# Spectral mixing in groups (0,1,2), (3), (4,5), (6,7), with its sums and the swapped weights' differences on VectorE instead of GpSimd

## The chip, the core and the metric

The kernel runs on one core of one Trainium2 chip. The metric is the time of one execution on the device. Before the change it is 1936.89 us, the median of three runs (1936.51 to 1940.29). Five engines work side by side, each through its own queue of instructions in order: TensorE (PE; its weight loads PEld stand apart in the profile), VectorE (DVE), ScalarE (ACT), GpSimd (POOL) and SyncE (SP), which here only issues DMAs.

## The reference

Three layers follow each other, on 8 batches of 576 tokens with 512 channels (4608 tokens in all):

```python
# layer 1: attention, keys and values averaged over 8 tokens
scores = scale * np.matmul(q, k_p.transpose(0, 1, 3, 2))
x = softmax(scores) @ v_p
# layer 2: mixing over tokens of rank 32, then two matmuls over channels
u = x + (x.T @ U @ V).T
x = u + np.maximum(u @ w_ch1, 0.0) @ w_ch2
# layer 3: real part of the FFT over tokens and channels, then again two matmuls
mixed = np.real(np.fft.fft(np.fft.fft(x, axis=1), axis=2))
u = x + mixed
un = (u - mean(u)) / np.sqrt(var(u) + 1e-06)
out = u + np.maximum(un @ w_ch1, 0.0) @ w_ch2        # other weights than layer 2
```

The weights come in as 64-bit floats.

## The kernel before

**Numbers in two parts.** A matmul operand is kept as a high part (rounded by ScalarE) and a low part (the difference). `split` (L105) does both: a copy on ScalarE, then the subtraction on VectorE, or on the engine it is given. So one product takes three matmuls.

**Stage one (to about 1095 us).** Attention for all batches, token mixing, and the channel layer of layer 2 in 18 blocks of 256 tokens (`st1`, `st2`, 16 slices `f` each, L1097 on). What a block finishes goes to the DRAM tensor `x1d`. TensorE's first matmul of a slice writes a bank `h0` or `h1`; VectorE then forms `low` (L917) and `hl` (L918) from it, and the bank is free again after `low`.

**Stage two (from about 1095 us).** The channel layer of layer 3, in 9 blocks of 512 tokens (`NBA`, L1207), each in 8 steps `p` (L1209) of seven products. Between the products `tick` (L1192) is called four times in every `p`. Each call steps two generators once: `d`, the spectral mixing, and `p`, the preparation of the next block. What they yield between two steps is thus put between the products in the program's order. In this stage the order of PE, DVE and ACT is the program's (L1098, L1206); before it a scheduler orders PE, DVE, POOL and SP.

**Spectral mixing (`Dft.run`, L523, called by `lane_d`, L1009).** One batch at a time, begun late in stage one (771 us) and ended in stage two (1526 us). Folded tokens: a batch's rows `F` and their mirror rows `R` are loaded in three tiles (`i` = 0, 1, 2); `S = F + R` on GpSimd (L562), then `R = F - R` and the edges `E` on VectorE. Matmuls with the tables `st` transform over tokens, those with `dt` over channels. A transformed tile goes into `S` and `E`, and four sums add it to rows loaded again (L676 to L679): two on GpSimd, two on VectorE. The result goes to the DRAM tensor `u2d`. A batch has two such output tiles of 128 rows and 33 rows that stay over. These are collected in `cath`, `catl`, `catp`, and the last batch of a group makes one further output tile of them (`n2 = 3`, L610). Only after the last batch of a group does `lane_d` say how far `u2d` goes:

```python
34    GROUPS = ((0, 1, 2), (3, 4), (5, 6, 7))
1014                  yield from df.run(b, group)
1015              state["u2"] = (group[-1] + 1) * S
```

**Preparation (`prep_a`, L765).** It loads four tiles of 128 tokens of `u2d` (`ul`), normalises each (VectorE, and GpSimd for the power, L790), transposes it on TensorE (L812), copies it back on ScalarE (L821), and splits it. In block `b`, `begin` (L1198) is asked at each `p` whether `u2` reaches to the end of block `b + 1`; only then is the preparation begun. At `p = 6` the program calls the generator again and again until it is used up, with nothing between (L1258), as the next block can't start without it.

**The swapped weights.** `w2` of layer 3 takes the place of `w2` of layer 2 at the end of stage one: `w_swap` (L246) loads one of 16 slices from `wd`, `w_swap_split` (L249) splits it, its difference on GpSimd. These are called by `swap` (L1082) in the last block of stage one and the first `p` of stage two. `ring_load` (L861) fetches the weights `wr` of the seven products.

Of the kernel before, what the change touches and what calls it, by code (L numbers as in the profile page):

```python
# [8 lines left out]
F32 = mybir.dt.float32  # L9
# [21 lines left out]
KSCALE = 1.0 / (POOL * 8)  # L31
NK = 290
NL = 258
GROUPS = ((0, 1, 2), (3, 4), (5, 6, 7))
NPR = NF // 2
TA = 512
NBA = NTOK // TA
# [7 lines left out]
def kernel(  # L45
# [18 lines left out]
    nc = tc.nc  # L64
# [25 lines left out]
    def bank(tag):  # L90
        return ps_b.tile([128, 512], F32, tag=tag, name=tag)
# [7 lines left out]
    def sub(eng, o, a, b):  # L99
        eng.tensor_tensor(out=o, in0=a, in1=b, op=ALU.subtract)  # L100

    def add(eng, o, a, b):
        eng.tensor_tensor(out=o, in0=a, in1=b, op=ALU.add)  # L103

    def split(hi, lo, src, eng=None):  # L105
        nc.scalar.activation(out=hi, in_=src, func=ACTF.Copy)  # L106
        sub(eng or nc.vector, lo, src, hi.bitcast(F32))

    def mm(o, a, b, start, stop):
        nc.tensor.matmul(o, a, b, start=start, stop=stop, skip_group_check=True)  # L110
# [137 lines left out]

    def w_swap_split(f):  # L249
        w = W[1, f]  # L250
        split(w[:, 0], w[:, 1], w[:, 1].bitcast(F32), nc.gpsimd)


    class Attn:
# [249 lines left out]
    class Dft:  # L504
# [18 lines left out]
        def run(self, b, group):  # L523
# [4 lines left out]
            def tl(tag, shape=(128, DM), dt=F32):  # L528
                return p1.tile(list(shape), dt, tag=tag, name=tag)
# [9 lines left out]
            def loads(i):  # L539
                f, r = tl("F"), tl("R")  # L540
                k0, n = KT[i]
                if i == 2:
                    for g in range(3):
                        nc.sync.dma_start(out=f[33 * g:33 * g + 33], in_=x1d[z + k0:z + k0 + 33, :])
                        nc.sync.dma_start(out=r[33 * g:33 * g + 32], in_=x1d[z + 288 + k0:z + S, :])
                        nc.sync.dma_start(out=r[33 * g + 32:33 * g + 33], in_=x1d[z + 288:z + 289, :])
                    return f, r, 99
                nc.sync.dma_start(out=f, in_=x1d[z + k0:z + k0 + n, :])
                mirror_in(r, i)
                return f, r, n  # L550
# [7 lines left out]
            for i in range(3):  # L558
                f, r, n = fr
                s = tl("S")  # L560
                e = tl("E")
                add(nc.gpsimd, s[:n], f[:n], r[:n])  # L562
                yield
                sub(nc.vector, r[:n], f[:n], r[:n])
                nc.gpsimd.tensor_copy(e[:n, 0:1], s[:n, 0:1])
                nc.gpsimd.memset(e[:n, 511:512], 0.0)
                sub(nc.vector, e[:n, 256:511], r[:n, 1:256], r[:n, 256:511])
                add(nc.vector, e[:n, 1:256], s[:n, 1:256], s[:n, 256:511])
                c2 = s[:n, 511:512].to_broadcast([n, 64])
                if i < 2:  # L570
                    fr = loads(i + 1)
                yield
                xe = tl(f"xe{i}", (128, 96 if i < 2 else 64), F32R)
                if i < 2:
                    xh, xl = tl(f"xh{i}", dt=F32R), tl(f"xl{i}", dt=F32R)
                    split(xh, xl, e)
                    nc.scalar.activation(out=xe[:, 0:64], in_=c2, func=ACTF.Copy)
                    sub(nc.vector, xe[:, 64:96], c2[:, 0:32], xe[:, 0:32].bitcast(F32))
                    X.append((xh, xl))
                    XE.append(xe)  # L580
                else:
                    m = self.sm
                    for h, y, w in ((xe, c2, 64), (None, e, 512)):
                        h = h or tl("S", dt=F32R)
                        q = r[:, 0:w]
                        nc.vector.tensor_scalar(out=q[:n], in0=y[:n], scalar1=m[:n, 0:1], scalar2=None, op0=ALU.mult)
                        nc.scalar.activation(out=h[:n], in_=y[:n], func=ACTF.Copy)
                        nc.vector.scalar_tensor_tensor(out=h[:n], in0=h[:n].bitcast(F32), scalar=m[:n, 1:2], in1=q[:n], op0=ALU.mult, op1=ALU.add)
                    X.append((h,))
                    XE.append(xe)  # L590
                yield
                if i < 2:
                    yield
                    yield
# [17 lines left out]
            def loads2(i):  # L612
                f, r = tl("F"), tl("R")
                if i < 2:
                    k0, n = KT[i]
                    nc.sync.dma_start(out=f[:n], in_=x1d[z + k0:z + k0 + n, :])
                    mirror_in(r, i)
                else:
                    n = 33 * len(group)
                    for j, zj in enumerate(y * S for y in group):  # L620
                        nc.sync.dma_start(out=f[33 * j:33 * j + 33], in_=x1d[zj + 256:zj + 289, :])
                        nc.sync.dma_start(out=r[33 * j:33 * j + 32], in_=x1d[zj + 544:zj + 576, :])
                        nc.sync.dma_start(out=r[33 * j + 32:33 * j + 33], in_=x1d[zj + 288:zj + 289, :])
                return f, r, n
# [23 lines left out]
            for i in range(n2):  # L648
                f, r, n = fr
                if i < 2:  # L650
                    k0 = KT[i][0]
                    ks = slice(k0, k0 + n)
                    Q = [(ph[:m, ks], pl[:m, ks], m) for ph, pl, m in P]
                    qx = px[:, ks]
                else:
                    hi, lo, qx = self.cat
                    Q = [(hi[:p[2], a, :n], lo[:p[2], a, :n], p[2]) for a, p in enumerate(P)]
                    qx = qx[:, :n]
                state["busy"] = True
                a, bb = bank("s0"), bank("s1")  # L660
                for c, o in ((0, a), (1, bb)):
                    for g in range(2):
                        ph, pl, m = Q[2 * c + g]
                        th, tl_ = self.dt[:m, c, g, 0], self.dt[:m, c, g, 1]
                        last = c == 1 and g == 1
                        mm(o[:n, 0:NL], ph, th, g == 0, False)
                        mm(o[:n, 0:NL], ph, tl_, False, False)
                        mm(o[:n, 0:NL], pl, th, False, last)
                mm(a[:n, 0:NL], qx, self.pt, False, True)
                s, e = tl("S"), tl("E")  # L670
                nc.scalar.activation(out=e[:n, 0:NL], in_=bb[:n, 0:NL], func=ACTF.Copy)
                sub(nc.vector, s[:n, 0:257], a[:n, 0:257], e[:n, 0:257])
                add(nc.vector, e[:n, 0:257], a[:n, 0:257], e[:n, 0:257])
                yield
                state["busy"] = False
                add(nc.gpsimd, f[:n, 0:256], f[:n, 0:256], s[:n, 0:256])  # L676
                add(nc.vector, f[:n, 256:512], f[:n, 256:512], e[:n, 1:257])
                add(nc.vector, r[:n, 0:256], r[:n, 0:256], e[:n, 0:256])
                add(nc.gpsimd, r[:n, 256:512], r[:n, 256:512], s[:n, 1:257])  # L679
                if i < 2:  # L680
                    nc.sync.dma_start(out=u2d[z + k0:z + k0 + n, :], in_=f[:n])
                if i == 0:
                    for a, m in ((1, 15), (16, 112)):
                        nc.sync.dma_start(out=u2d[z + 288 + a:z + 288 + a + m, :], in_=r[a:a + m])
                elif i == 1:
                    nc.sync.dma_start(out=u2d[z + 416:z + 544, :], in_=r)
                else:
                    for j, zj in enumerate(y * S for y in group):
                        nc.sync.dma_start(out=u2d[zj + 256:zj + 289, :], in_=f[33 * j:33 * j + 33])
                        nc.sync.dma_start(out=u2d[zj + 544:zj + 576, :], in_=r[33 * j:33 * j + 32])  # L690
                yield
                if i + 1 < n2:
                    fr = loads2(i + 1)
                    yield
                    yield
                    yield
# [312 lines left out]
    def lane_d(df):  # L1009
        for group in GROUPS:  # L1010
            for b in group:
                while state["x1"] < (b + 1) * S:
                    yield
                yield from df.run(b, group)
            state["u2"] = (group[-1] + 1) * S
# [32 lines left out]
    f = at.first()  # L1048
# [158 lines left out]
    for b in range(NBA):  # L1207
        begun = False
        for p in range(NPR):  # L1209
            x = ops[b]  # L1210
            n = 7 * (NPR * b + p)
# [157 lines left out]
```

## Time and profile before

| | before |
|---|---|
| median of 3 runs | 1936.89 us |
| the profiled execution | 1937.21 us, span 1935.4 us |
| PE busy | 1842.9 us (95%), 11239 matmuls |
| DVE busy | 1013.1 us (52%), 2281 instructions |
| ACT busy | 677.8 us (35%) |
| POOL busy | 250.4 us (13%), 387 instructions |
| DMA (q1) | 330.25 MB, 55.2% of 16 engines |
| mean granted TensorE clock | 0.985 of full speed |

The span is the time from the first to the last instruction; 1.8 us of the execution lie outside it. In the chain of work that ended last, PE has 61% of the span. In the profile's 40 slices (48.4 us each) PE's busy share is at 9 tenths or more but for four of the first five, the one from 1064 us (8) and the one from 1548 us (7); the granted clock is at 9 tenths or more but for the second (7) and the one from 1548 us (8).

### The profile page before, as it was taken

The page shows a single profiled execution, that of the slowest core. Times are in us where ns is not written, and L with a number is a line of the kernel's source. Part 1 is how long each engine was busy: PE and PEld are TensorE (multiplying, and loading weights), DVE is VectorE, ACT ScalarE, POOL GpSimd, SP SyncE. Part 2 cuts the span into 40 slices and gives each one's busy share as a digit, 9 for nine tenths or more (in the row PEclk, how much of TensorE's full clock was granted, in tenths as well). Part 3 has the DMA queues.
Part 4 walks back from the last instruction along what each step waited for, and adds up shares of the span by engine and source line. Part 5 has one row for each costly group of instructions (what it writes and reads, how often), then busy time and mean ns, then how long its engine had stood idle before and what let it go on. Part 6 is the DMA issues. An engine that isn't in the chain of part 4 may idle for free.

```text
span 1935.4 us, 31090 instructions
## 1 busy us (share of the span) xinstructions
PE 1842.9 (95%) x11239; PEld 1636.5 (85%) x11239; DVE 1013.1 (52%) x2281; ACT 677.8 (35%) x2115; POOL 250.4 (13%) x387
## 2 busy tenths in 40 slices
PE   5789899999999999999999899999999979999999
PEld 4578888898988888888888799889989968999998
DVE  8985454546454544444445755565655354444332
ACT  6553434343433432223232433333333233233221
POOL 3431011111100000111112511111111000000000
PEclk9799999999999999999999999999999989999999
DMA  9435464646453544432314758686867656757663
GB/s 363 168 124 168 137 196 142 194 134 206 121 181 108 146 118 129 117 88 57 87 49 131 251 183 260 194 266 192 252 214 247 195 153 196 238 178 226 186 211 131
DMA packets 255418, 335.64 MB, mean 173 GB/s; under 512 B 84576, under 2 KB 109248, under 8 KB 255264
## 3 DMA queue, kind: packets, MB, share of 16 engines
q1 hardware_dynamic: 254336, 330.25, 55.2%
q0 software_dynamic: 928, 3.40, 0.5%
q8 instruction: 89, 1.46, 0.3%
q14 instruction: 65, 0.53, 0.1%
HBM read 268.69 MB, written 64.88 MB: 172 GB/s over the span
## 4 chain that ended last, share of the span: by engine, by line
PE 61%; DMA 6%; DVE 4%; ACT 1%; issue 1%; SPq 1%; DVEq 0%; ACTq 0%
PE h L110 27%; PE o L110 19%; PE hu L110 5%; PE m L110 5%; PE s L110 3%; DMA cv<-w2b 3%; PE s L812 1%; DMA raw<-vr 0%; DVE hl L921 0%; DMA wr<-wc 0%; DVE xl L100 0%; DMA raw<-kT 0%; DMA ul<-u2d 0%; SPq L705 0%; DMA out<-ur 0%
## 5 line engine op out<-in xcount | busy, mean ns | idle before, releaser
L110 PE MATMUL h<-utx,w 128*128 128x256 f32 (+1 forms) x3048 | 478.8, 301 | 16.2 <-DVE hl L921 6.3
L110 PE MATMUL o<-w,hh 128*128 128x512 f32 x1632 | 478.8, 399 | 1.5 <-ACT hh L920 1.2
L110 PEld LDWEIGHTS h<-utx,w 128*128 128x128 f32 x3048 | 432.0, 192 | 56.7 <-DVE hl L921 9.9
L110 PEld LDWEIGHTS h<-x,wr 128*128 128x128 f32 x3024 | 398.0, 191 | 26.3 <-issue 2.5
L110 PE MATMUL h<-x,wr 128*128 128x256 f32 x3024 | 412.9, 284 | 5.7 <-DMA wr<-wc 2.1
L110 PEld LDWEIGHTS o<-w,hh 128*128 128x128 f32 x1632 | 289.2, 190 | 47.5 <-ACT hh L920 3.2
L110 PE MATMUL o<-w,hl 128*128 128x512 f32 x816 | 279.0, 397 | 2.5 <-DVE hl L921 2.5
L110 PEld LDWEIGHTS o<-w,hl 128*128 128x128 f32 x816 | 150.3, 190 | 28.6 <-DVE hl L921 3.8
L103 DVE TENSOR_TENSOR side<-h,side 128x256 f32<-128x256 f32 (+1 forms) x144 | 79.6, 553 | 125.7 <-PE h L110 124.3
L413 ACT ACTIVATE s<-s,mx 128x72 f32<-128x72 f32 x296 | 90.7, 332 | 69.6 <-DVE mx L410 69.5
L915 ACT ACTIVATE low<-h 128x256 f32<-128x256 f32 x102 | 39.2, 384 | 205.3 <-PE h L110 167.6
L1183 ACT ACTIVATE hh<-side 128x256 fp32r<-128x256 f32 (+1 forms) x144 | 75.0, 521 | 95.4 <-DVE side L103 88.0
L1183 ACT ACTIVATE hh<-h 128x256 fp32r<-128x256 f32 x72 | 27.6, 384 | 210.1 <-PE h L110 208.9
L1189 DVE SCALAR_TENSOR_TENSOR hl<-h,hh 128x256 fp32r<-128x256 f32 x72 | 30.5, 424 | 134.1 <-ACT hh L1183 134.1
L920 ACT ACTIVATE hh<-h 128x256 fp32r<-128x256 f32 x170 | 65.9, 387 | 97.3 <-PE h L110 88.2
L103 DVE TENSOR_TENSOR low<-h,low 128x256 f32<-128x256 f32 x102 | 42.8, 420 | 100.8 <-ACT hh L916 98.2
L1189 DVE SCALAR_TENSOR_TENSOR hl<-side,hh 128x256 fp32r<-128x256 f32 (+1 forms) x144 | 81.8, 568 | 25.1 <-ACT hh L1183 23.2
L921 DVE SCALAR_TENSOR_TENSOR hl<-h,hh 128x256 fp32r<-128x256 f32 x170 | 70.6, 415 | 34.8 <-ACT hh L920 34.3
L100 POOL TENSOR_TENSOR wo<-wo 128x256 fp32r<-128x256 f32 x56 | 43.3, 785 | 326.5 <-ACT wo L106 320.9
L110 PE MATMUL m<-w,hh 128*128 128x512 f32 x304 | 83.6, 394 | 0.0
L110 PE MATMUL hu<-w,hh 128*128 128x512 f32 x288 | 79.0, 396 | 0.0
L100 DVE TENSOR_TENSOR x<-ul,x 128x256 fp32r<-128x256 f32 x112 | 46.2, 448 | 38.5 <-ACT x L106 38.5
(254 smaller groups left out, 2423.4 us busy)
## 6 DMA issues: line engine op xcount, KB each, us to landing
wr<-wc SPq DMA_DIRECT2D x252, 512.0 KB
x<-x SPq DMA_DIRECT2D x56, 256.0 KB
wc<-wo SPq DMA_DIRECT2D x56, 256.0 KB
ur<-ud SPq DMA_DIRECT2D x36, 256.0 KB
x1d<-ur SPq DMA_DIRECT2D x36, 256.0 KB
ul<-u2d SPq DMA_DIRECT2D x36, 256.0 KB
ur<-u2d SPq DMA_DIRECT2D x36, 256.0 KB
out<-ur SPq DMA_DIRECT2D x36, 256.0 KB
```

The lines of the kernel that those rows point to most:

```text
L100: eng.tensor_tensor(out=o, in0=a, in1=b, op=ALU.subtract)
L103: eng.tensor_tensor(out=o, in0=a, in1=b, op=ALU.add)
L110: nc.tensor.matmul(o, a, b, start=start, stop=stop, skip_group_check=True)
L413: nc.scalar.activation(out=s[:n, a], in_=v[:, k], func=ACTF.Exp, bias=mx[:n, a:a + 1], accum_out=sm[:n, a:a + 1])
L812: nc.tensor.transpose(o[:, k * 128:k * 128 + 128], u[:, k * 128:k * 128 + 128], ident)
L915: nc.scalar.activation(out=low, in_=o[:, T:2 * T], func=ACTF.Copy)
L920: nc.scalar.activation(out=hh, in_=p, func=ACTF.Relu)
L921: nc.vector.scalar_tensor_tensor(out=hl, in0=p, scalar=0.0, in1=hh.bitcast(F32), op0=ALU.max, op1=ALU.subtract)
L1183: nc.scalar.activation(out=hh[:, i], in_=c, func=ACTF.Relu)
L1189: nc.vector.scalar_tensor_tensor(out=hl[:, i], in0=c, scalar=0.0, in1=hh[:, i].bitcast(F32), op0=ALU.max, op1=ALU.subtract)
```

## The change

Three edits. The mixing's groups are other ones, four in place of three: after a group's last batch `u2` now goes up after batch 2, 3, 5 and 7, where it went up after batch 2, 4 and 7. One batch more is the last of its group, so one output tile more is computed. The sum `S = F + R` and the two sums with `S` are given to VectorE, and so is the difference of the swapped weights.

```diff
-GROUPS = ((0, 1, 2), (3, 4), (5, 6, 7))
+GROUPS = ((0, 1, 2), (3,), (4, 5), (6, 7))
...
     def w_swap_split(f):
         w = W[1, f]
-        split(w[:, 0], w[:, 1], w[:, 1].bitcast(F32), nc.gpsimd)
+        split(w[:, 0], w[:, 1], w[:, 1].bitcast(F32))
...
                 s = tl("S")
                 e = tl("E")
-                add(nc.gpsimd, s[:n], f[:n], r[:n])
+                add(nc.vector, s[:n], f[:n], r[:n])
                 yield
                 sub(nc.vector, r[:n], f[:n], r[:n])
...
                 state["busy"] = False
-                add(nc.gpsimd, f[:n, 0:256], f[:n, 0:256], s[:n, 0:256])
+                add(nc.vector, f[:n, 0:256], f[:n, 0:256], s[:n, 0:256])
                 add(nc.vector, f[:n, 256:512], f[:n, 256:512], e[:n, 1:257])
                 add(nc.vector, r[:n, 0:256], r[:n, 0:256], e[:n, 0:256])
-                add(nc.gpsimd, r[:n, 256:512], r[:n, 256:512], s[:n, 1:257])
+                add(nc.vector, r[:n, 256:512], r[:n, 256:512], s[:n, 1:257])
```

What this moves is seen in the order of the instructions. First PE at `p = 6` of stage two's block 4, before. Rows with `wr` are the products, rows with `w,hh` and `w,hl` the second matmul, rows of L812 the transposes of the next block's preparation (four tiles of four).

```order
L110 MATMUL h_16522<-x_15092,wr 128x256 x6
L110 MATMUL o_16062<-w,hh 128x512 x4
L110 MATMUL o_16062<-w,hl 128x512 x2
L812 MATMUL s_16639<-ident,ul 128x128 x4
L812 MATMUL s_16655<-ident,ul 128x128 x4
L812 MATMUL s_16669<-ident,ul 128x128 x4
L812 MATMUL s_16682<-ident,ul 128x128 x4
L110 MATMUL h_16716<-x_15089,wr 128x256 x6
```

All four stand in a row, after them the first product of `p = 7`. Now the third of the four in the changed kernel, in the same block:

```order
L110 MATMUL h_16261<-x_15071,wr 128x256 x6
L110 MATMUL o_16077<-w,hh 128x512 x4
L110 MATMUL o_16077<-w,hl 128x512 x2
L812 MATMUL s_16385<-ident,ul 128x128 x4
L110 MATMUL h_16391<-x_15068,wr 128x256 x6
L110 MATMUL hu<-w,hh 128x512 x4
L110 MATMUL hu<-w,hl 128x512 x2
L110 MATMUL h_16392<-x_15476,wr 128x256 x6
```

The four are spread over block 4 from an earlier `p` on, each alone between products, as they stand in the blocks before and after it in both kernels.

Second, PE in block 0 of stage two in the changed kernel, where batch 3 is now the last of a group. `cath`, `catl`, `catp` hold the 33 rows, `s` are the two banks, `m` is the second matmul:

```order
L110 MATMUL m<-w,hh 128x512 x4
L110 MATMUL m<-w,hl 128x512 x2
L110 MATMUL s_12188<-dt,cath 33x258 x2
L110 MATMUL s_12188<-dt,catl 33x258
L110 MATMUL s_12188<-dt,cath 33x258 x2
L110 MATMUL s_12188<-dt,catl 33x258
L110 MATMUL s_12189<-dt,cath 33x258 x2
L110 MATMUL s_12189<-dt,catl 33x258
L110 MATMUL s_12189<-dt,cath 33x258 x2
L110 MATMUL s_12189<-dt,catl 33x258
L110 MATMUL s_12188<-pt,catp 33x258
L110 MATMUL h_12145<-x_11290,wr 128x256 x6
```

These 13 matmuls are new there; the tiles of the groups (4,5) and (6,7) take the place of those of (3,4) and (5,6,7).

Third, DVE near the end of stage one, before. `r` belongs to the preparation, `F`, `R`, `S`, `E` to the mixing, `low` to the channel layer:

```order
L100 TENSOR_TENSOR r_11073<-r_11207,r_11073 128x256
L100 TENSOR_TENSOR r_11073<-r_11073 128x256
L100 TENSOR_TENSOR R<-F,R 128x512
L103 TENSOR_TENSOR E<-S 128x255
L100 TENSOR_TENSOR E<-R 128x255
L103 TENSOR_TENSOR low<-h_11264,low 128x256
```

And now:

```order
L100 TENSOR_TENSOR r_11073<-r_11207,r_11073 128x256
L103 TENSOR_TENSOR S<-F,R 128x512
L100 TENSOR_TENSOR r_11073<-r_11073 128x256
L100 TENSOR_TENSOR R<-F,R 128x512
L103 TENSOR_TENSOR E<-S 128x255
L100 TENSOR_TENSOR w<-w 128x512
L100 TENSOR_TENSOR E<-R 128x255
L103 TENSOR_TENSOR low<-h_11264,low 128x256
```

Ahead of the same `low` stand two instructions more, the sum and one difference of the swapped weights. Elsewhere before stage two the scheduler's order of DVE changes by a few places; in stage two the sums stand where their generator yields them.

## Rows read from the trace of the kernel before

**Rows 1.** Windows of 50 us. Columns: stretch, us, busy (count) of each engine, clock, DMA.

```profile
1050.00:1100.00 50.00, 44.22 (x234) 37.20 (x233) 40.97 (x87) 25.64 (x67) 29.69 (x30) 0.97 0.67 210
...
1100.00:1150.00 50.00, 47.94 (x307) 43.76 (x306) 27.59 (x71) 15.89 (x39) 9.35 (x20) 0.97 0.59 203
...
1550.00:1600.00 50.00, 38.23 (x228) 33.56 (x228) 27.28 (x72) 14.65 (x36) 2.58 (x4) 0.90 0.55 168
```

**Rows 2.** Windows of 10 us, the one in the middle of the gap.

```profile
1560.00:1570.00 10.00, 3.76 (x18) 3.21 (x19) 3.37 (x12) 3.22 (x7) 0.00 (x0) 0.55 0.00 0
```

**Rows 3.** Chain of waits, 1520 to 1610 us: start, length, engine, output and line.

```profile
1537.90 1.39 PE m L110 x6
...
1548.47 1.39 PE m L110 x6
...
1555.81 0.56 DVE ul L806
1556.41 0.67 PE s L812 x4
...
1575.52 1.39 PE m L110 x6
...
1605.81 0.44 PE s L812 x4
```

**Rows 4.** Timeline of DVE, first output sum of blocks 2, 3, 4: start, length, instruction.

```profile
1379.80 0.68 DVE L103 TENSOR_TENSOR ur<-hu,ur 128x512 f32<-128x512 f32 x1
...
1475.42 0.69 DVE L103 TENSOR_TENSOR ur<-hu,ur 128x512 f32<-128x512 f32 x1 [0.57 <-PE hu L110]
...
1584.70 0.69 DVE L103 TENSOR_TENSOR ur<-hu,ur 128x512 f32<-128x512 f32 x1
```

**Rows 5.** Chain of waits of the whole span, the last group's output tile.

```profile
1519.39 1.57 PE s L110 x13
```

**Rows 6.** POOL's groups: operation, shapes, count, busy us, mean ns, idle before and releaser.

```profile
L103 POOL TENSOR_TENSOR S<-F,R 128x512 f32<-128x512 f32 (+1 forms) x24 | 31.9, 1330 | 66.0 <-DMA R<-x1d 60.4 <-DVE hl L1189 4.3 <-DVE xe L100 0.8
...
L100 POOL TENSOR_TENSOR w<-w 128x512 fp32r<-128x512 f32 x16 | 22.6, 1428 | 11.8 <-ACT w L106 11.8
L103 POOL TENSOR_TENSOR R<-R,S 128x256 f32<-128x256 f32 (+2 forms) x19 | 15.9, 835 | 0.0
L103 POOL TENSOR_TENSOR F<-F,S 128x256 f32<-128x256 f32 (+2 forms) x19 | 14.6, 769 | 182.3 <-DVE S L100 168.5 <-DVE mv L789 13.8
```

**Rows 7.** DVE on like shapes: a group by form, and tile F (least/median/most ns).

```profile
L100 DVE TENSOR_TENSOR xl<-x,xh 128x512 fp32r<-128x512 f32 x35 | 25.1, 717 | 5.7 <-ACT xh L106 5.6
...
L103 DVE TENSOR_TENSOR F<-F,E x19: 406/505/859, 841.5 to 1523.4; 128x256 f32<-128x256 f32 x16, 99x256 f32<-99x256 f32 x2, 66x256 f32<-66x256 f32 x1
```

**Rows 8.** Timelines of DVE, POOL and PE at the end of stage one.

```profile
1054.96 1.45 DVE L918 SCALAR_TENSOR_TENSOR hl<-low,hh 128x256 fp32r<-128x256 f32 x1
...
1079.34 3.12 POOL L100 TENSOR_TENSOR w<-w 128x512 fp32r<-128x512 f32 x2
...
1081.26 1.48 DVE L100 TENSOR_TENSOR E<-R 128x255 f32<-128x255 f32 x1
...
1083.13 2.93 PE L110 MATMUL h<-utx,w 128*128 128x512 f32 x8 [3.55 <-DVE low L103]
...
1087.51 1.55 PE L110 MATMUL h<-utx,w 128*128 128x512 f32 x8
...
1095.87 1.29 DVE L100 TENSOR_TENSOR xe<-S,xe 128x32 fp32r<-128x32 f32 x1
```

**Rows 9.** Tile F's waits, and timelines of POOL and DVE around two sums.

```profile
  DMA R<-x1d: 60.4, 13
...
779.48 0.69 DVE L100 TENSOR_TENSOR R<-F,R 128x512 f32<-128x512 f32 x1 [2.59 <-POOL S L103]
...
1156.30 1.29 POOL L103 TENSOR_TENSOR S<-F,R 128x512 f32<-128x512 f32 x1 [6.80 <-DMA R<-x1d]
...
1165.35 0.68 DVE L100 TENSOR_TENSOR R<-F,R 128x512 f32<-128x512 f32 x1
```

## The prediction, made blind

> **What bounds the kernel now.** I read the windows of 50 us first. PE is busy nearly all the time, so what ends the kernel is PE's work plus its gaps, and outside the start there are two groups of gaps in reach of the change [rows 1]. From 1550 to 1600 us PE is busy 38.23 us at a clock of 0.90. From 1050 to 1150 us it is busy 92.2 of 100, at 0.97, and there VectorE is loaded most: 40.97 of 50 us. Then I read the chain of waits inside each gap.
>
> The gap at 1550 is a chain VectorE, PE, ScalarE, VectorE, repeated for four tiles: normalise (L806), transpose (L812), copy, split [rows 3]. It is the preparation of block 5, run with nothing between its steps. Why there: block 5 needs tokens up to 3072. Before, `u2` goes from 2880 (batch 4) straight to 4608 (batch 7). Batch 7 ends in block 4's fifth step of eight, so `begin` says yes at the sixth, too late, and the loop at L1258 runs most of the preparation in one piece.
>
> **The groups.** Now `u2` reaches 3456 after batch 5, which the order places in block 2; block 5's preparation can begin with block 4. The quoted order of PE shows the transposes spread over block 4. What the gap costs: the same row of the second matmul (`m`) comes every 10.57 us in the quiet (1537.90 to 1548.47), but the next comes 27.05 us later, at 1575.52 [rows 3]. That is 16.48 us late. The transposes remain, 4 groups of 0.44 us as after the gap (1605.81), 1.76 us. Gain: 16.48 - 1.76 = 14.7 us. A second reading agrees in size: from the first output sum of block 2 to that of block 3 are 95.6 us, from there to that of block 4 109.3 us, though the mixing takes part in both stretches: 13.7 us [rows 4]. Within the 16.48 us lies the slow clock: 1560 to 1570 was granted 0.55, with PE busy 3.76 of the 10 us [rows 2], and even the first transposes take 0.67 us against 0.44 [rows 3]. Without the gap it should not fall; it is in the 16.48 us already.
>
> Does it only move? Blocks 3, 4 and 6 need 2048, 2560 and 3584 tokens. They now get them after batch 3, 5 and 7. Batch 5 is later than batch 4 was: the program has it done in the sixth step of block 2, nine calls of `tick` (24 us) ahead of block 3, where block 4's preparation begins. No four groups of transposes stand in a row any more. Cost of this: nothing.
>
> The price is one more output tile: 13 matmuls, 1.57 us on PE by the last such tile [rows 5], all on the path. Its DMAs are the same small ones by batch, issued earlier or later on SP by some steps; its instructions on VectorE are counted below. So +1.6 us.
>
> **The sums and differences on VectorE.** GpSimd loses 24 sums `S`, 16 differences and two times 19 sums, 31.9 + 22.6 + 15.9 + 14.6 = 85 us [rows 6]. On VectorE these take: `S` 24 x 0.69 (the same shape, 779.48 in [rows 9]) = 16.6 us; differences 16 x 0.72 = 11.5 us; 40 sums (20 tiles now) x 0.41, the least of `F<-F,E`, = 16.4 us [rows 7]. Together 44.5 us over some 450 us of stage two and 320 us of stage one, where VectorE is half idle. Against it stands what it gets back. Between 1054.96 and 1095.87 eleven of its instructions, the first and the last of them in [rows 8], are longer than their like, by 10.9 us in all: the one at 1081.26 takes 1.48 us where its like takes 0.42, and it ends as the GpSimd instructions that begin at 1079.34 end. `F<-F,E` beside a GpSimd sum has a median of 505 ns against 406.
>
> The Trainium skill, in SBUF — State Buffer, section Who interferes with whom, says that a VectorE instruction with two SBUF inputs and a GpSimd instruction that reads SBUF lock each other out for a whole instruction. By that rule these 10.9 us go with the GpSimd work; the rows above fit it. The Trainium skill, in Perfetto Trace Analysis, section Optimizing Scalar/DVE Operations, says on the other side that work of a saturated VectorE may well go to GpSimd, and adds that this may not help as the two share a port. By its first half alone the change is wrong at 1050 to 1100 us; that is the second rival.
>
> At that place the edit counts most. All 16 differences fall between 1054 and 1101 us: added 16 x 0.72 + 3 x 0.69 = 13.6 us, returned 10.9. So VectorE is as full as before. For PE one burst matters. PE waits 3.55 us for `low` at 1083.13 and its 8 matmuls then take 2.93 us against 1.55 when warm, 4.9 us lost [rows 8]. Ahead of that `low`, in the quoted order, one `r`, `E` and `E` lose about 1.05 us each, and `S` and one difference come in, 1.41 us: `low` is 1.7 us earlier. I take a gain of 2 us (bounds: 4.9 gained if the wait and the slow matmuls go, 2.7 lost if the surplus of 13.6 over 10.9 all reaches PE; nearest to the burst's own 1.7).
>
> **The wait that is added.** Today GpSimd stands 60.4 us, 13 times, before `S` until the rows `R` have landed [rows 9]. Now VectorE stands there, with `low` and `hl`, or `side` and `hl`, queued behind it, and PE waits for those. But GpSimd comes to that place early because it has little else. VectorE comes later: in stage two `S` begins at 1156.30, as the rows land, and VectorE's own next instruction of that tile begins at 1165.35; one `tick` (2.6 us, a quarter of 10.57) ahead of that is where `S` now stands, 6 us behind the landing. In stage one VectorE already waits, by way of GpSimd (2.59 us at 779.48): there it gains. Bounds: 0, and some 1 us at each of the six sums in stage one that now stand ahead of a `low`. I take 0.5 us lost. In stage two PE has next to no gaps before 1550 and VectorE is 60% busy; four sums in a row are 1.7 us in place of two of about 0.5 to 0.86: 0.
>
> **Sum**, against the profiled execution: 1937.2 - 14.7 + 1.6 - 2 + 0.5 = 1922.6 us. The median of the runs is 0.3 us below that execution: 1922 us.
>
> **Rivals.**
> 1. VectorE hands on its load. If the long instructions have another cause than GpSimd, 13.6 us of work come into a stretch that is 82% busy, of which 9 us are free; some 4.6 us reach PE there: 1937.2 - 13.1 + 4.6 = 1929 us; with a tenth of the other 31 us, spread over the mixing, 1932. For it: the 3.55 us wait has this form already. Against: the ends that coincide in [rows 8].
> 2. Slower than before: VectorE takes over GpSimd's wait for `R`. If it stood there as GpSimd does, 60.4 us, and PE bore it all, the time were 1937.2 - 13.1 + 60 = 1984 us. It decides from 13.1 us on, which is 1.0 us for each of 13 waits. Against it the 6 us of margin above; for it only that rows load behind other DMAs on SP.
> 3. The change doesn't do what it says: the gap moves to block 3 or returns as a wait for `u2d` at the start of a preparation. Then only the tile is left, and the switch: 1937.2 + 1.6 - 2 = 1937. Against: the order, and nine calls of `tick` between the stores and the loads.
> 4. More is gained: all of PE's gaps from 1050 to 1150 (7.8 us idle) go with the locks: 1937.2 - 13.1 - 7.8 = 1916, or a little less with the clock.
>
> **Chances.** Forecast (1918 to 1927) 0.70; rival 4 (1914 to 1918) 0.10; rival 1 (1927 to 1932) 0.12; rival 3 0.04; rival 2 0.04. The range 1914 to 1931 holds the first three nearly whole. A measurement of this kernel tells about 0.2%, 3.9 us, from no change: faster 0.92, same 0.04, slower 0.04.
>
> **What would show it.** Right: no window of 10 us between 1500 and 1600 with PE under 9 us; the chain there holds products and L812 rows alone; the spacing of the first output sums of blocks 3 and 4 about 95 us; VectorE instructions of 1.4 us and more gone from 1054 to 1096, and a wait under 2 us in place of 3.55. Wrong: VectorE's `S` with an idle time put down to the DMA of `R` and PE waiting for `side`, `hl` or `low` behind it; four L812 rows with idle PE between them in any block; PE busy under 44 of 50 us at the switch.

## The result

| | median (range, runs) | ratio to before |
|---|---|---|
| before, timed beside it | 1938.59 us (1936.51 to 1941.53, 4) | |
| changed | 1917.41 us (1913.93 to 1924.2, 4) | 0.9894 [0.9863, 0.9925] |
| changed, timed again (below) | 1924.35 us (1922.14 to 1926.56, 5) | 0.992 [0.9907, 0.9933] |

Each ratio is to the kernel before as timed beside it (a median of 1938.59 us, and of 1940.17 us for the second time). The changed kernel is faster by about 1%. The forecast of 1922 us lies between its two medians. Its profiled execution took 1924.2 us, with a span of 1922.4 us and a mean clock of 0.989. The first section of its page gives busy time by engine:

```profile
PE 1840.7 (96%) x11252; PEld 1633.1 (85%) x11252; DVE 1024.2 (53%) x2365; ACT 676.6 (35%) x2116; POOL 173.3 (9%) x309
```

PE's busy time hardly fell (1842.9 before), though 13 matmuls came in: the time came out of its gaps. VectorE has 84 instructions more and only 11.1 us more busy time. GpSimd lost 77.1 us. The windows of 50 us show the same places as [rows 1], with the same columns (1.00 behind the counts is the full clock):

```profile
1050.00:1100.00 50.00, 46.27 (x248) 38.09 (x247) 43.29 (x116) 26.67 (x71) 6.00 (x9) 1.00 0.71 220
1100.00:1150.00 50.00, 47.46 (x311) 43.14 (x310) 27.64 (x75) 15.51 (x39) 4.73 (x14) 1.00 0.65 211
...
1550.00:1600.00 50.00, 50.00 (x318) 45.20 (x317) 21.99 (x54) 13.50 (x36) 2.57 (x4) 1.00 0.71 227
```

The gap at 1550 is closed: PE 50.00 us of 50 at full clock, against 38.23 at 0.90. At 1050, PE has 2.05 us more; at 1100, 0.48 less. The window of [rows 2] is full:

```profile
1560.00:1570.00 10.00, 10.00 (x65) 9.05 (x64) 2.69 (x7) 2.82 (x9) 0.00 (x0) 1.00 0.59 172
```

So are the nine others from 1500 to 1600 us. The four groups of transposes of block 5's preparation (L812) have products between them now. PE's timeline from 1500 to 1535 us:

```profile
1501.58 0.60 PE L812 MATMUL s<-ident,ul 128*128 128x128 f32 x4
...
1512.08 0.60 PE L812 MATMUL s<-ident,ul 128*128 128x128 f32 x4
...
1524.66 0.60 PE L812 MATMUL s<-ident,ul 128*128 128x128 f32 x4
...
1532.85 0.60 PE L812 MATMUL s<-ident,ul 128*128 128x128 f32 x4
```

The same marks as in [rows 4], VectorE's first output sums of blocks 2, 3 and 4:

```profile
1381.06 0.68 DVE L103 TENSOR_TENSOR ur<-hu,ur 128x512 f32<-128x512 f32 x1
...
1475.51 0.69 DVE L103 TENSOR_TENSOR ur<-hu,ur 128x512 f32<-128x512 f32 x1
...
1571.69 0.69 DVE L103 TENSOR_TENSOR ur<-hu,ur 128x512 f32<-128x512 f32 x1
```

From mark to mark are 94.5 and 96.2 us, where it was 95.6 and 109.3. At the switch of stages, VectorE and PE where [rows 8] stood:

```profile
1080.24 0.68 DVE L100 TENSOR_TENSOR w<-w 128x512 fp32r<-128x512 f32 x1
1080.84 0.42 DVE L100 TENSOR_TENSOR E<-R 128x255 f32<-128x255 f32 x1
1081.17 0.42 DVE L103 TENSOR_TENSOR low<-h,low 128x256 f32<-128x256 f32 x1
...
1081.64 1.68 PE L110 MATMUL h<-utx,w 128*128 128x512 f32 x8 [1.02 <-DVE low L103]
```

The edge sum `E<-R` takes 0.42 us (1.48 before) although a difference of 0.68 us stands ahead of it. PE waits 1.02 us for `low` instead of 3.55, and its eight matmuls take 1.68 us instead of 2.93.

**Where the time came from, by stage.** I compared each profile with that of before between fixed marks, the first output sum (`ur`) of a block. That gives the table below, in us, negative is faster. The marks at either end of its second column, before and then changed, in VectorE's timelines (what runs ahead of 751 us is the same code in both kernels):

```profile
751.30 0.68 DVE L103 TENSOR_TENSOR ur<-o,ur 128x512 f32<-128x512 f32 x1
...
1041.25 0.69 DVE L103 TENSOR_TENSOR ur<-o,ur 128x512 f32<-128x512 f32 x1 [0.99 <-PE o L110]
```

```profile
752.37 0.68 DVE L103 TENSOR_TENSOR ur<-o,ur 128x512 f32<-128x512 f32 x1
...
1043.62 1.29 DVE L103 TENSOR_TENSOR ur<-o,ur 128x512 f32<-128x512 f32 x2 [1.56 <-PE o L110]
```

| profile of | to 751 | 751 to 1041 | 1041 to 1093 (switch) | block 0, to 1189 | blocks 1 to 3, to 1475 | block 4, to 1585 | sum from 751 |
|---|---|---|---|---|---|---|---|
| before, again | +1.0 | 0.0 | +0.5 | -2.3 | +0.1 | 0.0 | -1.7 |
| changed | +1.1 | +1.3 | -2.9 | +1.0 | -0.4 | -13.1 | -14.1 |
| changed, again | +5.6 | +0.7 | -4.1 | -0.3 | -1.5 | -13.1 | -18.3 |
| groups only | +2.6 | 0.0 | +1.6 | +1.3 | -0.8 | -12.7 | -10.6 |
| engines only | +3.5 | +0.4 | -3.8 | -2.2 | -1.2 | +0.5 | -6.3 |
| swapped difference only | +1.1 | +0.1 | -2.5 | -0.4 | 0.0 | +0.5 | -2.3 |
| sums only | +6.2 | +0.9 | -2.4 | -1.4 | -1.2 | 0.0 | -4.1 |
| groups (3,4,5), (6,7) | +4.1 | +1.0 | -4.4 | -2.9 | +32.3 | -24.2 | +1.8 |
| first weights too | -8.0 | +0.8 | -4.1 | -0.7 | -0.7 | -13.1 | -17.8 |

The first column is noise, except in the last row, where alone that code differs: the others spread over 6.2 us, and two profiles of the changed kernel by 4.5 us. Block 0 spreads over some 4 us; there PE waits for the first weights `wr` of stage two (0.92 to 2.54 us). Differences of the first and fourth column are not read as effects below.

### The profile page after: what moved, and what is told of

Read it like the earlier page. It is cut to its first block, busy times and chain, and to the rows that moved or that the text cites. A ratio compares the mean times of both kernels' runs of the same rounds, so it can differ in the third digit from the quotient of the medians.

```text
span 1922.4 us, 30977 instructions
## 1 busy us (share of the span) xinstructions
PE 1840.7 (96%) x11252; PEld 1633.1 (85%) x11252; DVE 1024.2 (53%) x2365; ACT 676.6 (35%) x2116; POOL 173.3 (9%) x309
## 5 line engine op out<-in xcount | busy, mean ns | idle before, releaser
L110 PE MATMUL h<-utx,w 128*128 128x256 f32 (+1 forms) x3048 | 479.6, 302 | 14.3 <-DVE hl L921 5.9
L413 ACT ACTIVATION_READ_ACCUMULATOR s<-s,mx 128x1 f32 x296 | 64.5, 218 | 0.0
```

The source lines that it names most:

```text
L413: nc.scalar.activation(out=s[:n, a], in_=v[:, k], func=ACTF.Exp, bias=mx[:n, a:a + 1], accum_out=sm[:n, a:a + 1])
```

## The experiments

**The same program again**, for the size, and the kernel before for the spread of one profile. No edit in either.

> The changed kernel once more, for its spread and a second profile. My theory (a gap of 14.7 us before block 5 goes, one output tile of 1.6 us comes, about 3 us gained at the end of stage one, nothing elsewhere): 15 to 17 us under the kernel before, ratio 0.991 to 0.992. Rival (the engines' part brings as much as the groups', spread over the mixing): 20 us or more, ratio 0.9895 or less, as the four runs so far have it.

Measured 1924.35 us, ratio 0.992 [0.9907, 0.9933], with the intervals of the two measurements overlapping.

> The kernel before, unchanged, for a second profile. All profiles of the variants reach 751 us's mark (a point ahead of any changed instruction) 1.1 to 5.6 us later than the first profile of before. My theory: that first profile was early by chance, and this one reaches it 1 to 5 us later and takes 1938 to 1942 us. Rival (the variants are slower there for a reason): it comes within 1 us of the first, 751 and 1937.

One execution: 1936.42 us. Its mark at 751 came 1.0 us after that of the first profile, which is what the rival said: the first profile was not an early one by much. Why the unchanged first 751 us spread over 6 us stays open.

**The groups alone.**

```diff
-GROUPS = ((0, 1, 2), (3, 4), (5, 6, 7))
+GROUPS = ((0, 1, 2), (3,), (4, 5), (6, 7))
```

> The kernel before with the groups (0,1,2), (3), (4,5), (6,7) alone; sums and differences stay on GpSimd. My theory: 14.7 - 1.6 = 13.1 us faster, ratio 0.9932; no gap between 1540 and 1580 us, the wait for low of 3.5 us near 1083 us stays. Rival (half of the gain belongs to the engines): 8 to 10 us faster, ratio 0.995 to 0.996.

Measured 1930.43 us (1927.99 to 1931.57, 5 runs), ratio 0.9952 [0.9939, 0.9964]: 9.3 us gained, with an interval of 7.0 to 11.8 us that leaves out the 13.1 I had expected and holds the 8 to 10 of the rival. The stages show that the gap did go: block 4 is shorter by 12.7 us. From 751 us on the one profile has 10.6 us, as block 0 with the added tile and the switch are longer. Some of that is in block 0, where GpSimd does the sums of the tile that was added. POOL, DVE and PE there:

```profile
1164.82 1.30 POOL L103 TENSOR_TENSOR F<-F,S 33x256 f32<-33x256 f32 x1 [13.85 <-DMA wr<-wc]
...
1165.56 2.09 DVE L100 TENSOR_TENSOR ul<-ul 128x256 f32<-128x256 f32 x3
...
1168.04 1.69 PE L110 MATMUL h<-x,wr 128*128 128x256 f32 x12 [1.26 <-DVE side L103]
```

and in the changed kernel, with those sums on VectorE:

```profile
1161.40 1.34 DVE L100 TENSOR_TENSOR ul<-ul 128x256 f32<-128x256 f32 x3
...
1163.13 1.70 PE L110 MATMUL h<-x,wr 128*128 128x256 f32 x12 [0.46 <-DVE side L103]
```

Three differences take 2.09 us beside GpSimd and 1.34 us without it; `side` is late by so much, and PE waits 1.26 instead of 0.46 us. So the edits touch each other, by 0.8 us here.

**The engines alone**, with the old groups: the three sums and the difference of L251 on VectorE (the next two diffs together).

> The old groups, sums and differences on VectorE. My theory: 2 to 3 us faster, ratio 0.9985, all of it at the end of stage one; the gap of about 15 us in block 4 stays. Rival (the engines bring half of it): 8 us or more faster, ratio 0.996 or less. Rival (VectorE hands on its load): slower by 2 us or more.

Measured 1935.5 us (1934.29 to 1939.31, 11 runs), ratio 0.9982 [0.9973, 0.999], which is 3.5 us. The gap is there, at its old place (window 1560 to 1570, columns as in [rows 2]):

```profile
1560.00:1570.00 10.00, 5.89 (x22) 5.02 (x23) 4.99 (x16) 2.86 (x6) 0.00 (x0) 0.52 0.10 25
```

The switch is shorter by 3.8 us: PE's burst of [rows 8] (the eight matmuls into `h`) waits 0.16 us and takes 1.68.

```profile
1082.33 1.68 PE L110 MATMUL h<-utx,w 128*128 128x512 f32 x8 [0.16 <-DVE low L103]
```

The product of the two ratios, 0.9952 x 0.9982 = 0.9934, lies just above the interval of the changed kernel timed again, [0.9907, 0.9933]. Whether the two edits together give a little more than their sum is left open.

**The difference alone, and the sums alone.**

```diff
-        split(w[:, 0], w[:, 1], w[:, 1].bitcast(F32), nc.gpsimd)
+        split(w[:, 0], w[:, 1], w[:, 1].bitcast(F32))
```

> The kernel before with the differences of the swapped weights alone on VectorE. My theory (what the engines bring is VectorE's freedom from GpSimd's long instructions at the end of stage one): 3 us faster, ratio 0.9985; from the first output sum before 1041 us to the one at 1093 us some 3.5 us less; VectorE's instructions of 1.4 us there gone but for those beside the three sums S; the gap in block 4 stays. Rival (the sums bring it): no change within 1 us.

```diff
-                add(nc.gpsimd, s[:n], f[:n], r[:n])
+                add(nc.vector, s[:n], f[:n], r[:n])
...
-                add(nc.gpsimd, f[:n, 0:256], f[:n, 0:256], s[:n, 0:256])
+                add(nc.vector, f[:n, 0:256], f[:n, 0:256], s[:n, 0:256])
...
-                add(nc.gpsimd, r[:n, 256:512], r[:n, 256:512], s[:n, 1:257])
+                add(nc.vector, r[:n, 256:512], r[:n, 256:512], s[:n, 1:257])
```

> The kernel before with the spectral mixing's sums alone on VectorE; swapped weights stay on GpSimd, old groups. My theory: no change within 2 us, ratio 0.999 to 1.001; the wait for low of about 3 us near 1083 us stays. Rival (the sums bring most): 3 us or more faster. Rival (VectorE hands on its load, or waits for R): 2 us or more slower.

The difference alone: 1936.67 us (11 runs), ratio 0.9982 [0.997, 0.9994], 3.5 us where 3 were expected. The sums alone: 1936.53 us (11 runs), ratio 0.9983 [0.9975, 0.9992]. Each shortens the switch by about 2.4 us, and both together not by 4.8 but by 2.9 to 4.1. PE's timeline at the burst, of the difference alone and then of the sums alone:

```profile
1081.81 2.87 PE L110 MATMUL h<-utx,w 128*128 128x512 f32 x8 [1.90 <-DVE low L103]
```

```profile
1085.71 1.68 PE L110 MATMUL h<-utx,w 128*128 128x512 f32 x8 [0.41 <-DVE low L103]
...
1088.35 0.73 PE L110 MATMUL o<-w,hl 128*128 128x512 f32 x2 [0.97 <-DVE hl L918]
```

With the difference alone the wait falls to 1.90 us, but the matmuls behind it stay slow; with the sums alone both go, and a wait for `hl` appears. The slow matmuls run at a lower clock. Windows around the burst in the kernel before, behind its wait of 3.55 us, and with the difference alone, behind 1.90:

```profile
1083.00:1086.00 3.00, 2.87 (x9) 2.49 (x10) 2.96 (x10) 1.83 (x7) 0.00 (x0) 0.51 0.75 239
```

```profile
1081.80:1084.80 3.00, 2.99 (x9) 2.61 (x10) 3.00 (x9) 1.61 (x6) 0.00 (x0) 0.52 0.84 252
```

The granted clock is about half there, the lower of TensorE's two levels (1.2 and 2.4 GHz). In the changed kernel, behind 1.02 us, it stays at 1.00. With the sums alone GpSimd still has the differences, but here its next two begin after `low` (VectorE's at 1085.24 us), and the long VectorE instructions are now an `x` (1.31 us) and `hl`:

```profile
1085.33 2.69 POOL L100 TENSOR_TENSOR w<-w 128x512 fp32r<-128x512 f32 x2
...
1086.81 1.49 DVE L918 SCALAR_TENSOR_TENSOR hl<-low,hh 128x256 fp32r<-128x256 f32 x1
```

So the differences cost PE less here because they fall at another time; that any order would do so is not shown. For the sums alone I had expected no change within 2 us; 3.3 us [1.6, 4.9] came. That was a miss.

**The gap put elsewhere.** This keeps the changed engines and lets `u2` rise after batches 2, 5 and 7, so that block 3 is short of tokens.

```diff
-GROUPS = ((0, 1, 2), (3,), (4, 5), (6, 7))
+GROUPS = ((0, 1, 2), (3, 4, 5), (6, 7))
```

> The changed kernel with three groups, (0,1,2), (3,4,5), (6,7): the last group is as in the changed kernel, the count of output tiles as in the kernel before. My theory: block 5 has its tokens in time, but block 3 needs batch 3, which now counts only with batch 5, done at the sixth step of block 2: the gap stands at the end of block 2 (near 1360 us) in place of block 4, about 15 us long, and the time is that of the run with old groups and the engines changed, within 3 us. Rival (the gain comes from the smaller last group, 6 and 7, or from the spectral mixing itself): as fast as the changed kernel or 1.6 us faster for the tile saved.

Measured 1942.93 us (1940.0 to 1948.34, 12 runs), ratio 1.0019 [1.0008, 1.0029]. Block 4's window is full, and one in block 2 is not (columns as in [rows 2]):

```profile
1370.00:1380.00 10.00, 5.87 (x23) 4.87 (x22) 6.05 (x16) 3.82 (x9) 1.57 (x5) 0.50 0.18 52
...
1560.00:1570.00 10.00, 10.00 (x64) 8.96 (x63) 5.68 (x14) 3.35 (x10) 0.00 (x0) 1.00 0.76 205
```

PE's timeline in that gap has the transposes (L812), and beside them the mixing's matmuls with `st`, each waiting for VectorE:

```profile
1369.37 1.09 PE L812 MATMUL s<-ident,ul 128*128 128x128 f32 x4 [3.17 <-DVE ul L806]
...
1374.41 0.61 PE L110 MATMUL s<-st,S 99*128 99x290 f32 x1 [2.50 <-DVE S L588]
```

So `u2` does decide where the gap lies. It is larger here: mixing that would have run beside products runs in it, which the stages show as +32.3 us in blocks 1 to 3 and -24.2 in block 4. With that, and against my expectation, the kernel is some 7 us slower than with the old groups and the same engines.

**More work from GpSimd to VectorE: the first weights.** In the changed kernel the low parts of the weights that are read first (`done` in `w_first`) are still differences on GpSimd. VectorE is busy 45.97 of 50 us from 50 to 100 us, so this is the strongest test of whether VectorE hands on its load.

```diff
-                split(w[:, 0], w[:, 1], ts[f][k].bitcast(F32), nc.gpsimd)
+                split(w[:, 0], w[:, 1], ts[f][k].bitcast(F32))
```

> The changed kernel, and the first weights' 32 differences too on VectorE (45 us of GpSimd from 20 to 200 us, where VectorE is busy 41 to 46 of 50 us and PE waits). It asks whether a move to VectorE pays where VectorE is fullest. My theory (VectorE gives up to GpSimd's instruction as long as it lasts: two TENSOR_SCALAR take 2.90 us beside it, 0.75 alone): the same to 4 us faster than the changed kernel, ratio 0.990 to 0.992. Rival (a full VectorE only gets fuller by 32 x 0.7 = 22 us): 5 us or more slower than the changed kernel, ratio 0.9945 or more.

Measured 1911.47 us (1909.98 to 1914.14, 4 runs), ratio 0.9857 [0.9841, 0.9873], the fastest kernel here: more than the 4 us beyond the changed kernel that I had allowed for. And once more:

> The changed kernel with the first weights' differences on VectorE, once more, on the same chip as the run with both. My theory: 10 to 13 us faster than the changed kernel, ratio 0.985 to 0.987 as the time before. Rival (the 12 us were one chip's): ratio 0.989 or more.

1913.46 us (1912.75 to 1917.37, 4 runs), 0.9879 [0.9863, 0.9896], between the 0.987 expected at most and the 0.989 of the rival. Against the changed kernel's ratios, 0.9894 and 0.992, that is a further gain of 3 to 12 us; the two kernels were not timed side by side, and some of the intervals overlap. The stage is clearer. The mark of the first column stands at 743.27 and 744.61 us in these two profiles, and at 751.30 to 757.49 us in the nine without a change ahead of it. Windows of the changed kernel, then of this one:

```profile
50.00:100.00 50.00, 37.31 (x191) 29.29 (x191) 45.97 (x75) 27.38 (x69) 21.47 (x19) 0.82 0.47 156
100.00:150.00 50.00, 43.82 (x252) 36.95 (x252) 40.03 (x76) 29.54 (x94) 18.80 (x15) 0.93 0.41 133
...
0.00:200.00 200.00, 150.65 (x856) 125.81 (x857) 152.38 (x279) 102.81 (x333) 63.95 (x74) 0.92 0.60 202
```

```profile
50.00:100.00 50.00, 37.12 (x189) 29.82 (x190) 49.94 (x97) 29.94 (x86) 10.67 (x5) 0.80 0.55 187
100.00:150.00 50.00, 47.47 (x294) 41.99 (x294) 43.30 (x93) 31.73 (x100) 7.77 (x12) 0.97 0.54 167
...
0.00:200.00 200.00, 157.05 (x901) 131.43 (x901) 152.54 (x318) 105.54 (x346) 26.03 (x42) 0.93 0.62 207
```

In 200 us VectorE runs 39 instructions more in the same busy time, and PE 45 matmuls more. From 50 to 100 us VectorE does become full (49.94 us) and PE does no better; from 100 to 150 us PE is busy 3.65 us more. The groups by form up to 210 us tell how (count, busy us, mean ns, idle before), again changed first:

```profile
L129 DVE SCALAR_TENSOR_TENSOR scr<-wraw,scr 128x512 int32<-128x512 int32 x28 | 24.0, 875 | 0.1
...
L124 DVE TENSOR_SCALAR scr<-wraw 128x512 int32<-128x512 int32 x28 | 19.3, 713 | 0.0
...
L100 POOL TENSOR_TENSOR w<-scr,w 128x512 fp32r<-128x512 f32 x28 | 40.5, 1459 | 48.7 <-ACT w L106 48.7
```

```profile
L100 DVE TENSOR_TENSOR w<-scr,w 128x512 fp32r<-128x512 f32 x28 | 18.5, 678 | 0.0
L129 DVE SCALAR_TENSOR_TENSOR scr<-wraw,scr 128x512 int32<-128x512 int32 x28 | 18.3, 676 | 0.0
L124 DVE TENSOR_SCALAR scr<-wraw 128x512 int32<-128x512 int32 x28 | 10.7, 415 | 0.0
```

A difference that took GpSimd 1459 ns takes VectorE 678, and two of VectorE's own operations on the same weights fall, the shift (L124) from 713 to 415 ns and the one of L129 from 875 to 676. These two give back 14.3 us of the 18.5 that the differences add.

**And the weights that are stored.** The same edit also in `put`.

```diff
-            split(o[:, 0], o[:, 1], raw_of(o), nc.gpsimd)
+            split(o[:, 0], o[:, 1], raw_of(o))
```

> The changed kernel with the first weights' 32 differences and the second weights' 56 differences on VectorE too. The 56 fall between 180 and 560 us, take 44 us on GpSimd, and there VectorE is half idle and PE waits some 20 us in all for it. My theory (VectorE gets back about what it takes on): the same as with the first weights' differences alone to 4 us faster, ratio 0.9835 to 0.986. Rival (a half idle VectorE had room beside GpSimd, so the 56 only lengthen its queue ahead of xl and hl): 2 us or more slower than with the first weights' alone, ratio 0.987 or more.

1915.46 us (1910.96 to 1917.96, 4 runs), 0.9881 [0.9865, 0.9897], beside 0.9879 without it: no further gain that these runs can tell, where I had expected 0.986 at most. The mark at 751 stands at 749.10 us in its profile, 4.5 and 5.8 us later than in the two without this edit. That points to the rival, but it is one profile, and the totals don't tell the two kernels apart.

## Why the prediction was right

**The gap, -14.7 us, and the tile, +1.6: right, and shown.** Block 4 is shorter by 13.1 us in both profiles, and by 12.7 with the groups alone; with the engines alone the gap stays. The added tile is not in this block, so the 13.1 us stand against the term of 14.7 alone. But the mixing has 7 matmuls more in this block than before, and 7 fewer in blocks 1 to 3. Block 4 between its marks (us, busy time and count of each engine), before and then changed:

```profile
1475.42:1584.70 109.28, 97.51 (x611) 87.72 (x610) 45.86 (x111) 29.85 (x73) 9.21 (x17) 0.95 0.59 184
```

```profile
1475.51:1571.69 96.18, 95.82 (x618) 86.96 (x617) 49.90 (x126) 30.03 (x76) 4.68 (x14) 1.00 0.67 218
```

Blocks 1 to 4 together are shorter by 13.5 and 14.6 us, so the term was at most 1.2 us too large. The added tile is in block 0; PE's timeline has its first matmul and the product behind its last:

```profile
1158.12 0.41 PE L110 MATMUL s<-dt,cath 128*33 128x258 f32 x2
...
1159.68 1.60 PE L110 MATMUL h<-x,wr 128*128 128x256 f32 x12
```

That is 1.56 us, against 1.57. Rival 3 (the gap only moves) is out: blocks 2 to 4 are alike (95.6, 94.5 and 96.2 us). The run with groups (3,4,5), (6,7) shows that it could have happened: without a group for batch 3 alone the gap comes in block 2, larger.

**The switch, -2: the mechanism right, the size too small.** Measured -2.9 and -4.1 us, and -3.8 with the engines alone. Of the two bounds, the upper one (4.9 gained) was nearer. The term counted 1.7 us by which `low` comes earlier; but the wait fell by 2.5 us (in the second profile it is gone), and the slow matmuls behind it went too (2.93 to 1.68 us), as the clock did not fall. No single VectorE instruction from 1050 to 1100 us takes 1 us any more. The rule of the Trainium skill that the prediction set beside such rows (SBUF — State Buffer, Who interferes with whom: a VectorE instruction with two SBUF inputs and a GpSimd instruction that reads SBUF exclude each other) holds here: `E<-R` is 1.48 us beside GpSimd and 0.42 us without.

**Rival 1 (VectorE hands on its load, 1929 to 1932): out.** (The prediction's text once calls it the second rival; it is the first of its list.) VectorE is fuller from 1050 to 1100 (43.29 of 50 us, 40.97 before), and PE waits less. The prediction said "as full as before", though its own numbers, 13.6 us added and 10.9 returned, make it 2.7 us fuller. In the whole kernel VectorE's busy time grew by 11.1 us where the prediction added up 44.5 us of new work. The first weights on VectorE show the same over a fuller stretch, 0 to 200 us. The Trainium skill says that work of a saturated VectorE may go to GpSimd, and that this might not help, as the two share a read port (Perfetto Trace Analysis, Optimizing Scalar/DVE Operations); in both places here the opposite move paid.

**Rival 4 (all gaps from 1050 to 1150 go, 1916): out as a mechanism.** PE's idle time there is still 6.3 us, from 7.8. The first median, 1917.41, lies in this rival's span (1914 to 1918) all the same, and not in the forecast's own (1918 to 1927); the second, 1924.35, lies in the forecast's.

**The added wait, +0.5: of the right size, but little of it is shown to be the wait.** What waits for `R`, and tile F's sums after the change (least/median/most ns, and the idle time by releaser):

```profile
L103 DVE TENSOR_TENSOR S<-F,R x24: 679/684/693, 779.2 to 1478.9; 128x512 f32<-128x512 f32 x16, 99x512 f32<-99x512 f32 x8
...
L103 DVE TENSOR_TENSOR F<-F,E x20: 408/417/421, 842.7 to 1539.9; 128x256 f32<-128x256 f32 x16, 66x256 f32<-66x256 f32 x2, 99x256 f32<-99x256 f32 x1, 33x256 f32<-33x256 f32 x1
...
  DMA R<-x1d: 10.0, 5
```

VectorE waits 10.0 us in 5 places where GpSimd waited 60.4 us in 13 [rows 9]: it comes later, as argued, and rival 2 (1984) is out. `F<-F,E` has a median of 417 ns, from 505. One wait reaches PE, in stage one of the first profile:

```profile
958.78 0.69 DVE L103 TENSOR_TENSOR S<-F,R 128x512 f32<-128x512 f32 x1 [3.61 <-DMA R<-x1d]
...
960.93 1.68 PE L110 MATMUL h<-utx,w 128*128 128x512 f32 x8 [0.46 <-DVE low L103]
```

Of 3.61 us of waiting, PE sees 0.46. In the second profile the same sum waits 3.02 us, and PE none. From 751 to 1041 us the kernels with the sums on VectorE lose 0.4 to 1.3 us, and those without 0.1 at most. But PE's idle time between these marks is 0.46 us in the first profile and nothing in the second or with the engines alone, so the rest of the loss is in PE's busy time; in both profiles of the changed kernel two matmuls more lie between the marks (1559, from 1557). What else makes it up stays open.

**The mixing in stage two, 0: right within what can be told.** Blocks 1 to 3 change by -0.4 and -1.5 us, block 0 within its spread.

**The sum.** From 751 us on, 14.1 and 18.3 us were gained, against 14.6 forecast. Luck has a part in it: the gap's term was up to 1.2 us too large, and the switch's 0.9 to 2.1 too small. As whole executions the two profiles are 13.0 and 12.7 us shorter than the one before, as the unchanged code ahead of 751 us took 1.1 and 5.6 us longer in them. The executions behind the first median (1913.93 to 1917.49 us) left no profile, so where they gain a further 7 to 10 us is not shown.

## What to carry to other kernels

An engine's busy time is not its work: beside GpSimd's sums and differences part of VectorE's busy time here was waiting, and the work taken back from GpSimd cost VectorE little or nothing. Look for one operation on one shape with two durations before you call VectorE full. And where a preparation runs in one piece, look for the counter that lets it start: raising it two batches earlier for one block was worth 13 us in that block, at 1.6 us for the added matmuls in another, while raising it two batches later for another block made a larger gap there.

## What the runs showed of the hardware that I had not expected

- Not only VectorE's sums of two tensors are longer beside GpSimd: a shift with one tensor operand (L124) takes 713 ns beside GpSimd's differences and 415 without. So VectorE took over 32 of these differences at no cost in busy time (152.38 and 152.54 us).
- Gains at one place don't add: 2.5 and 2.4 us at the switch for each edit alone, 2.9 to 4.1 for both together. TensorE's clock takes part in this: it was granted at 0.52 in the burst with the difference alone, and at 1.00 with both.
- The same unchanged code, in the same order, took up to 6.2 us longer, in 751 us, from one profile to the next. Effects of a few us are told by stage, from marks within one execution, or by many runs, and not by two profiles.
